# Linear-attention block with a gated MLP: keys of three chunks computed by features and transposed back by DMA

## The chip, the cores and the metric

The kernel runs on one core of a Trainium2 chip. The metric is the device time of one execution in microseconds (us). Engines: TensorE (PE) multiplies matrices into eight PSUM banks, VectorE (DVE), ScalarE (ACT) and GpSimd (POOL) do elementwise work, SyncE (SP) issues most DMAs. Each engine, and each DMA queue, takes its instructions in the order in which the program lists them; an instruction that waits holds up all behind it.

## The reference: what is computed

x has 2048 rows (tokens) of 640 features in bf16. The matmul operands are bf16 throughout.

```python
xn = layernorm(x)
# A: linear attention, 32 heads of 20 features
q, k, v = split(xn @ wqkv)
phi = lambda t: jnp.where(t > 0, t + 1, jnp.exp(t)) + 1e-6
pq, pk = phi(q), phi(k)
kv = einsum("bhsd,bhse->bhde", pk, v);   z = einsum("bhsd->bhd", pk)
num = einsum("bhqd,bhde->bhqe", pq, kv); den = einsum("bhqd,bhd->bhq", pq, z)[..., None] + 1e-6
s = (num / den) @ wo
# B: MLP, 640 -> 1728 -> 640
g = silu(relu(xn @ w1) @ w2)
out = x + s * g
```

## The kernel before

**Tiling.** Tokens stand in 16 tiles of 128 and in 4 chunks of 512 (J=4); features in 5 blocks of 128 (C=5); the MLP's 1728 hidden features in 13 blocks and one of 64. `xn` holds the normalised x by tokens, `xnT` its transpose by features, `pk` phi(k) by tokens, `pqT` phi(q) by features.

**Scheduling.** `Sched` keeps one list of operations per engine in program order and works out semaphore waits from the keys that each operation reads (R) and writes (W). A group of matmuls waits for all its inputs ahead of its first matmul. DMAs go to the queue named (nearly all to SP), also in program order. The order is written out by hand; there is no planner.

**Stage 0 (chunk 0).** x tiles are loaded and centred, transposed by PE into `xnT`, and the MLP's first hidden blocks are computed (`H_first`, `H_mm` L547, evicted by ACT in `H_ev` L554). The list `order` (L690) mixes key tiles ("K", 0..7), that is, chunks 0 and 1, with hidden blocks 5 to 12. Tiles from 4 on are normalised on DVE (`LN_stats`: statistics L397 and L399, inverse root on POOL L401 and L403; `LN_norm` L412) and transposed by an SP DMA (`xnT_dma` L455).

**A key tile** is `K_mm` (L464): ten matmuls, five blocks of features times two halves of 320 columns, into two banks. Then an exponential (L482, L485) and a relu (L491 to L499) of 640 columns, mostly on ACT, and two passes on DVE in `K_fin` (L505, L507), which write `pk[:, t, :]`. `z_add` (L473) adds each `pk` tile to `zacc` on POOL.

**The chunk loop j = 1, 2, 3 (L711).** For chunk j it computes five query blocks (`Q_block`: PE L532, ACT exponential L539, DVE pair L540 and L542) and 13 hidden blocks, in the order q h h q h h ... for j = 1 and 2: 18 blocks, n = 0 to 17. Both need `xnT` of chunk j. For chunk j+1 it does `LN_stats` after n = 0, 2, 4, 6, `LN_norm` and the transpose after n = 1, 3, 5, 7, and a key tile after n = 9, 12, 14, 17 into banks 0 and 1. Queries and hidden blocks take banks 2 to 7 in a ring (`nextb`). Loop j=3 also does chunk 0's queries from a second transpose of xn (`xq0`, L746, into the place of the key weights), sums z over tokens on PE (`z_split`, `z_col` L637), makes the block-diagonal `zmat` and the denominators (`den`, L650 to L658).

**After the loop.** SP issues, in this order: w2 (L766, L770), the reciprocals to DRAM (L773), their replicas back (L777, five loads of 512 KB). PE computes the key-feature product `G_block` (L792), GT = xn^T pk: five blocks of 32 matmuls of 320 columns, evicted by ACT (L797). `kv_block` (L803) multiplies the value weights by GT, after five matmuls of the MLP's second layer (`T_main`, L844); `W_block` (L814) folds in wo. `divide` (L783) divides `pqT` on DVE. The rest is the second MLP layer, the products with `wf` (L887, L922), silu and the output.

Of the kernel before, what the change touches and what calls it, by code (L numbers as in the profile page):

```python
# [211 lines left out]
def bass_recurrent_scan__linear_attn_block__dense_activation_relu__prompt_kernel(  # L212
# [87 lines left out]
    zmat = nc.alloc_sbuf_tensor("zmat", [P, C, H], bf)  # L300
    zacc = nc.alloc_sbuf_tensor("zacc", [P, D], f32)
    zhl = nc.alloc_sbuf_tensor("zhl", [P, 2, D], bf)
    mhalf = nc.alloc_sbuf_tensor("mhalf", [P, 1], f32)
# [12 lines left out]
    def ps2(b, n):  # L316
        return psT[:, 512 * b:512 * (b + 2)].rearrange("p (a n) -> p a n", a=2)[:, :, 0:n]

    done_sems = {E: nc.alloc_semaphore(f"done_{E}") for E in CENGS}
    NDS = 100  # L320
    dma_sems = [nc.alloc_semaphore(f"dsem{i}") for i in range(NDS)]
# [29 lines left out]
    sc.op("POOL", lambda eng: eng.memset(mhalf[:, :], -0.5), W=[("mhalf",)])  # L351
    sc.op("POOL", lambda eng: eng.memset(zacc[:, :], 0.0), W=[("zacc",)])

# [54 lines left out]
    def xnk(t, cs=range(C)):  # L408
        return [("xn", t, c) for c in cs]

    def LN_norm(t):
        last_norm[0] = sc.op("DVE", lambda eng: eng.tensor_scalar(  # L412
            out=xn[:, t, :], in0=xin[:, t % XR, :], scalar1=mv[:, t, 0:1], scalar2=rsy[:, t:t + 1],
            op0=ALU.subtract, op1=ALU.mult), R=[("xin", t % XR), ("mv", t), ("rsy", t)], W=xnk(t))
        if t + XR < T:
            x_load(t + XR)
# [51 lines left out]

    zpend = []

    def z_add():
        t = zpend.pop(0)
        sc.op("POOL", lambda eng: eng.tensor_tensor(out=zacc[:, :], in0=zacc[:, :], in1=pk[:, t, :], op=ALU.add),  # L473
              R=[("zacc",), ("pk", t)], W=[("zacc",)])

    def two(ap):
        return ap.rearrange("p (a n) -> p a n", a=2)

    def K_exp(t, b):
        e_ = two(ek[:, t % NEK, 0, :])  # L480
        if t < 4:
            sc.op("ACT", lambda eng: eng.activation(out=e_, in_=ps2(b, HN), func=ACTF.Exp, scale=rsy[:, t:t + 1]),  # L482
                  R=[("ps", b), ("ps", b + 1), ("rsy", t)], W=[("ek_e", t % NEK)])
        else:
            sc.op("ACT", lambda eng: eng.activation(out=e_, in_=ps2(b, HN), func=ACTF.Exp),  # L485
                  R=[("ps", b), ("ps", b + 1)], W=[("ek_e", t % NEK)])

    def K_relu(t, b):
        r_ = two(ek[:, t % NEK, 1, :])
        if t < 2:  # L490
            sc.op("DVE", lambda eng: eng.tensor_scalar(out=r_, in0=ps2(b, HN), scalar1=rsy[:, t:t + 1], scalar2=0.0,  # L491
                                                       op0=ALU.mult, op1=ALU.max),
                  R=[("ps", b), ("ps", b + 1), ("rsy", t), ("ek_e", t % NEK)], W=[("ek_r", t % NEK)])
        elif t < 4:
            sc.op("ACT", lambda eng: eng.activation(out=r_, in_=ps2(b, HN), func=ACTF.Relu, scale=rsy[:, t:t + 1]),
                  R=[("ps", b), ("ps", b + 1), ("rsy", t)], W=[("ek_r", t % NEK)])
        else:
            sc.op("ACT", lambda eng: eng.activation(out=r_, in_=ps2(b, HN), func=ACTF.Relu),  # L498
                  R=[("ps", b), ("ps", b + 1)], W=[("ek_r", t % NEK)])  # L499

    def K_fin(t):
        es = t % NEK
        e_ = ek[:, es, 0, :]
        r_ = ek[:, es, 1, :]
        sc.op("DVE", lambda eng: eng.tensor_scalar(out=e_, in0=e_, scalar1=1.0, scalar2=1e-6, op0=ALU.min, op1=ALU.add),  # L505
              R=[("ek_e", es)], W=[("ek_e", es)])
        sc.op("DVE", lambda eng: eng.tensor_tensor(out=pk[:, t, :], in0=e_, in1=r_, op=ALU.add),  # L507
              R=[("ek_e", es), ("ek_r", es)], W=[("pk", t)])
        zpend.append(t)

    def K_ev(t, b):
        K_exp(t, b)
        K_relu(t, b)
        K_fin(t)

# [3 lines left out]
    def nextb():  # L519
        b = RB[ring[0] % len(RB)]  # L520
        ring[0] += 1
        return b
# [106 lines left out]

    def z_split():  # L630
        sc.op("POOL", lambda eng: eng.tensor_copy(zhl[:, 0, :], zacc[:, :]), R=[("zacc",)], W=[("zhi",)])
        sc.op("POOL", lambda eng: eng.tensor_tensor(out=zhl[:, 1, :], in0=zacc[:, :], in1=zhl[:, 0, :], op=ALU.subtract),
              R=[("zacc",), ("zhi",)], W=[("zlo",)])

    def z_col():
        b = nextb()
        sc.group("PE", [(lambda eng, c=c, a=a: eng.matmul(ps[b][:, c:c + 1], lhsT=zhl[:, a, P * c:P * (c + 1)],  # L637
                                                          rhs=onesM[:, 0:1], start=(a == 0), stop=(a == 1)))
                        for c in range(C) for a in range(2)],
                 R=[("zhi",), ("zlo",), ("onesM",)], W=[("ps", b)])  # L640
        sc.op("DVE", lambda eng: eng.tensor_tensor(out=zmat[:, :, :], in0=mh[:, :, :],
                                                   in1=ps[b][:, 0:C].unsqueeze(2).to_broadcast([P, C, H]), op=ALU.mult),
              R=[("ps", b), ("mh",)], W=[("zmat",)])

# [18 lines left out]
    def K_step(t):  # L663
        b = (0, 6)[t % 2]
        K_mm(t, b)
        K_exp(t, b)
        if t == 0:
            LN_stats(4)
        K_relu(t, b)
        if t == 0:  # L670
            LN_norm(4)
            xnT_dma(4)
        if t == 1:
            LN_stats(5)
            K_fin(0)
            LN_norm(5)
            xnT_dma(5)
        if t >= 4:
            if t == 4:
                LN_norm(0)  # L680
                LN_norm(1)
            else:
                K_fin(t - 1)
            if t == 6:
                LN_norm(2)
                LN_norm(3)
            if t == 7:
                K_fin(t)

    order = [("K", 0), ("K", 1), 5, ("K", 2), 6, ("K", 3), 7, 8, ("K", 4), 9, ("K", 5), 10, ("K", 6), 11, ("K", 7), 12]  # L690
    for a in order:
        if isinstance(a, tuple):
            K_step(a[1])
        else:
            H_block(0, a, (2, 3, 4, 5)[(a - 5) % 4])
        if a == 6:
            LN_stats(6)
            K_fin(1)
            LN_norm(6)
            xnT_dma(6)  # L700
        if a == 8:
            LN_stats(7)
            K_fin(2)
            LN_norm(7)
            xnT_dma(7)
            K_fin(3)
    ring[0] = 0
    w_load(wv_sb[:, :, :], A_wqkv[:, 2 * D:3 * D], ("wv",))


    for j in range(1, J):  # L711
# [11 lines left out]
        for n, (kind, jj, f) in enumerate(blocks):  # L723
# [4 lines left out]
            if j + 1 < J:  # L728
# [3 lines left out]
                if n in (1, 3, 5, 7):  # L732
                    LN_norm(t0 + n // 2)
                    xnT_dma(t0 + n // 2)
                if n in (9, 12, 14, 17):
                    t = t0 + (9, 12, 14, 17).index(n)
                    K_mm(t, 0)
                    K_ev(t, 0)
                if n in (8, 10, 12, 14, 16):
                    z_add()  # L740
                if j == 1 and n == 16:
                    build_masks()
            else:
                if n == 0:
                    for t in range(4):
# [6 lines left out]
                        W=[("wo", 1)], extra=[last_norm[0]])  # L752
                if n % 2 == 0 and zpend:
                    z_add()
                    if not zpend:
                        z_split()
                if n == 18:
                    z_col()
                if n == 20:
                    den()  # L760
                    H_halves()
    assert not zpend

# [22 lines left out]


    def G_block(k, b):
        fns = []
        for t in range(T):  # L790
            for a in range(2):
                fns.append(lambda eng, t=t, a=a: eng.matmul(  # L792
                    ps[b + a][:, 0:HN], lhsT=xn[:, t, P * k:P * (k + 1)], rhs=pk[:, t, HN * a:HN * (a + 1)],
                    start=(t == 0), stop=(t == T - 1)))
        ag = sc.group("PE", fns, R=[kk for t in range(T) for kk in xnk(t)] + [("pk", t) for t in range(T)],
                      W=[("ps", b), ("ps", b + 1)])
        sc.op("ACT", lambda eng: eng.activation(out=two(GT[:, k, :]), in_=ps2(b, HN),  # L797
                                                func=ACTF.Copy), R=[("ps", b), ("ps", b + 1)], W=[("GT", k)])
        return ag

    def kv_block(c, b):
        n0 = V0[c]
        sc.group("PE", [(lambda eng, k=k: eng.matmul(ps[b][0:VR, 0:VR], lhsT=wv_sb[:, k, n0:n0 + VR],  # L803
                                                     rhs=GT[:, k, n0:n0 + VR], start=(k == 0), stop=(k == C - 1)))
                        for k in range(C)], R=[("wv",)] + [("GT", k) for k in range(C)], W=[("ps", b)])
        sc.op("DVE", lambda eng: eng.tensor_tensor(
# [142 lines left out]

    lastG = None  # L950
    for k in range(C):
# [117 lines left out]
```

## Time and profile before

| | |
|---|---|
| median of 3 runs | 221.4 us (220.67 to 221.53) |
| profiled execution, its own time | 220.62 us |
| its span | 218.9 us |
| PE clock granted | 1.00 |
| HBM read, written | 15.75 MB, 5.24 MB |

A row of a timeline is: start in us, length in us, engine, line of the code, operation, what it writes and reads, how many; in brackets how long the engine stood idle before and what released it. A row of the chain is start, length, engine and line. A group row is the line, engine and operation, the count, then busy time in us and mean ns of one. "DMA to landing" counts from the issue to the arrival of the last byte; x1, x2 or x5 is the number of issues. A matmul's own length is modelled and overlaps the next one's; the spacing in the chain is what it costs.

### The profile page before, as it was taken

Reading aid. Unit: us, or ns where it says so; the run is one execution under the profiler, and the core shown is the slowest. Engines: PE = TensorE matmul, PEld = TensorE weight load, DVE = VectorE, ACT = ScalarE, POOL = GpSimd, SP = SyncE. Lnnn points to the kernel's source line nnn. Section 1 sums busy time; section 2 is a strip of 40 time slices with the busy share of each in tenths; the row PEclk is TensorE's granted clock in tenths of the full one; section 3 lists DMA queues with packets and bytes.
Section 4 is the critical chain, followed back from the end, with each engine's and each line's share of the span. In section 5 each row is a group of like instructions: output and inputs, shape, how many; then the busy total and the mean of one; then the engine's idle time right before and its main releaser. Section 6 shows DMA issues by size and latency. Waiting matters only on the chain.

```text
span 218.9 us, 3262 instructions
## 1 busy us (share of the span) xinstructions
PE 214.4 (98%) x1318; PEld 118.3 (54%) x1318; DVE 113.9 (52%) x199; ACT 88.0 (40%) x147; POOL 43.5 (20%) x66
## 2 busy tenths in 40 slices
PE   7999999999999999999999999999999999999994
PEld 2975654555545554444467777534444446555573
DVE  2788846789676999987700006601121122460363
ACT  3587765567656666555321113614210311001120
POOL 2153101279023998700000000000000000000001
PEclk9999999999999999999999999999999999999999
DMA  6999581331013206800069959369212113342151
GB/s 205 294 377 189 121 240 36 61 54 8 0 30 60 33 1 120 168 3 0 0 194 364 275 172 371 90 206 316 48 24 48 24 27 73 76 157 89 38 180 63
DMA packets 36972, 26.46 MB, mean 121 GB/s; under 512 B 19973, under 2 KB 36317, under 8 KB 36957
## 3 DMA queue, kind: packets, MB, share of 16 engines
q1 hardware_dynamic: 36012, 25.50, 42.4%
q10 hardware_dynamic: 944, 0.75, 1.0%
q8 instruction: 10, 0.16, 0.3%
q14 instruction: 6, 0.04, 0.1%
HBM read 15.75 MB, written 5.24 MB: 96 GB/s over the span
## 4 chain that ended last, share of the span: by engine, by line
PE 96%; DMA 1%; DVE 1%; issue 0%
PE psT L547 26%; PE psT L844 19%; PE psT L464 10%; PE psT L792 10%; PE psT L532 10%; PE psT L887 7%; PE psT L851 7%; PE psT L922 2%; DMA reg<-in_A_x_dram 1%; PE psT L569 1%; PE psT L866 1%; PE psT L803 1%; PE psT L814 1%; PE psT L439 1%; PE psT L650 1%; DVE ek L426 0%
## 5 line engine op out<-in xcount | busy, mean ns | idle before, releaser
L547 PE MATMUL psT<-reg 128*128 128x512 bf16 (+1 forms) x335 | 61.7, 331 | 0.0
L844 PE MATMUL psT<-hT,reg 128*128 128x512 bf16 x195 | 44.6, 379 | 0.0
L547 PEld LDWEIGHTS psT<-reg 128*128 128x128 bf16 x335 | 28.5, 98 | 25.6 <-issue 0.4
L554 ACT ACTIVATE hT<-psT 128x512 bf16<-128x512 f32 x52 | 30.7, 600 | 15.8 <-PE psT L547 15.7
L894 DVE TENSOR_TENSOR er<-psT,ek 128x512 bf16<-128x512 f32 x15 | 10.4, 691 | 49.0 <-PE psT L887 49.0
L844 PEld LDWEIGHTS psT<-hT,reg 128*128 128x128 bf16 x195 | 18.9, 98 | 22.2 <-issue 0.7
L882 ACT ACTIVATE ek<-psT 128x512 bf16<-128x512 f32 x15 | 8.3, 599 | 42.3 <-PE psT L869 21.9
L929 POOL TENSOR_TENSOR reg<-reg 128x256 bf16<-128x256 bf16 x1 | 0.7, 666 | 123.8 <-DVE reg L937 123.8
L532 PE MATMUL psT<-reg 128*128 128x512 bf16 x100 | 24.9, 379 | 0.0
L464 PE MATMUL psT<-reg 128*128 128x320 bf16 x160 | 24.2, 299 | 0.0
L473 POOL TENSOR_TENSOR zacc<-zacc,reg 128x640 f32<-128x640 f32 x16 | 23.7, 1483 | 1.9 <-DVE reg L507 1.0
L792 PE MATMUL psT<-reg 128*128 128x320 bf16 x160 | 21.9, 299 | 0.0
L464 PEld LDWEIGHTS psT<-reg 128*128 128x128 bf16 x160 | 15.6, 98 | 8.2
L792 PEld LDWEIGHTS psT<-reg 128*128 128x128 bf16 x160 | 15.6, 98 | 6.2
L887 PE MATMUL psT<-pqT,reg 128*128 128x512 bf16 x75 | 18.1, 379 | 0.0
L542 DVE SCALAR_TENSOR_TENSOR pqT<-er 128x512 bf16<-128x512 bf16 x20 | 17.1, 854 | 0.7
L532 PEld LDWEIGHTS psT<-reg 128*128 128x128 bf16 x100 | 9.7, 98 | 11.6 <-DVE er L540 0.6
L539 ACT ACTIVATE er<-psT 128x512 bf16<-128x512 f32 x20 | 12.0, 598 | 8.9 <-PE psT L532 8.1
L851 PE MATMUL psT<-reg,hT 128*128 128x320 bf16 x104 | 15.3, 299 | 0.0
L540 DVE TENSOR_SCALAR er<-psT 128x512 bf16<-128x512 f32 x20 | 13.6, 678 | 3.1 <-ACT er L539 3.1
L507 DVE TENSOR_TENSOR reg<-ek 128x640 bf16<-128x640 bf16 x16 | 13.5, 843 | 1.5 <-ACT ek L498 1.0
L397 DVE BATCH_NORM_STATS2 stats<-reg 128x6 f32<-128x320 bf16 x32 | 13.9, 476 | 0.1
(71 smaller groups left out, 164.9 us busy)
## 6 DMA issues: line engine op xcount, KB each, us to landing
rscr<-rden SPq DMA_DIRECT2D x4, 640.0 KB, 10.5
reg<-rscr SPq DMA_DIRECT2D x5, 512.0 KB, 5.8
reg<-in_A_x_dram SPq DMA_DIRECT2D x4, 640.0 KB, 6.2
reg<-in_A_x_dram SPq DMA_DIRECT2D x15, 160.0 KB, 3.8
out_dram<-reg SPq DMA_DIRECT2D x15, 160.0 KB, 1.9
reg<-in_A_wqkv_dram SPq DMA_DIRECT2D x2, 800.0 KB, 6.6
reg<-in_B_w_dram SPq DMA_DIRECT2D x1, 1120.0 KB, 6.0
reg<-in_B_w_dram SPq DMA_DIRECT2D x1, 960.0 KB, 9.2
```

The source lines that it names most:

```text
L397: sc.op("DVE", lambda eng, a=a: eng.bn_stats(stats[:, t, a, :], xv[:, HN * a:HN * (a + 1)]), R=[("xin", t % XR)], W=[("stats", t, a)])
L464: fns.append(lambda eng, a=a, k=k: eng.matmul(ps[b + a][:, 0:HN], lhsT=xnT[:, k, tok(t)], rhs=wqk[:, k, D + HN * a:D + HN * (a + 1)], star ...
L473: sc.op("POOL", lambda eng: eng.tensor_tensor(out=zacc[:, :], in0=zacc[:, :], in1=pk[:, t, :], op=ALU.add), R=[("zacc",), ("pk", t)], W=[( ...
L532: sc.group("PE", [(lambda eng, k=k: eng.matmul(ps[b], lhsT=wqk[:, k, P * f:P * (f + 1)], rhs=rhs(k), start=(k == 0), stop=(k == C - 1))) f ...
L540: sc.op("DVE", lambda eng: eng.tensor_scalar(out=r_, in0=ps[b], scalar1=0.0, scalar2=1e-6, op0=ALU.max, op1=ALU.add), R=[("ps", b), ("er_e ...
L542: sc.op("DVE", lambda eng: eng.scalar_tensor_tensor(out=pqT[:, f, schunk(j)], in0=e_, scalar=1.0, in1=r_, op0=ALU.min, op1=ALU.add), R=[(" ...
L547: return sc.group("PE", [(lambda eng, k=k: eng.matmul(ps[b][:, lo:hi], lhsT=w1_sb[:, k, P * f:P * (f + 1)], rhs=xnT[:, k, 512 * j + lo:512 ...
L554: sc.op("ACT", lambda eng: eng.activation(out=hT[:, f, schunk(j)], in_=ps[b], func=ACTF.Relu), R=[("ps", b)], W=[("hT", j, f)])
L792: fns.append(lambda eng, t=t, a=a: eng.matmul(ps[b + a][:, 0:HN], lhsT=xn[:, t, P * k:P * (k + 1)], rhs=pk[:, t, HN * a:HN * (a + 1)], sta ...
L844: sc.group("PE", [(lambda eng, f=f: eng.matmul(ps[b], lhsT=w2_sb[:, f, P * m:P * (m + 1)], rhs=hT[:, f, schunk(j)], start=(f == 0 and not ...
L851: sc.group("PE", [(lambda eng, f=f: eng.matmul(ps[b][:, 0:HN], lhsT=hT[:, f, tok(t)], rhs=w2_sb[:, f, HN * n:HN * (n + 1)], start=(f == 0 ...
L887: sc.group("PE", [(lambda eng, c=c: eng.matmul(ps[b], lhsT=wf[:, c, P * m:P * (m + 1)], rhs=pqT[:, c, schunk(j)], start=(c == 0), stop=(c ...
```

## The change

Keys of chunk 0 stay as tiles by tokens. Keys of chunks 1 to 3 are computed by features: `KT_block(j, m)` multiplies the key weights of 128 features by 512 tokens of `xnT` (five matmuls of 512 columns, one bank of banks 0 and 1), takes phi there and sends the block back to token order in `pk` by a DMA transpose on SP. Since a feature's tokens now lie along a row, ACT sums them for z while copying (`K_sum`); chunk 0's keys are transposed by DMA into a part of `pqT` that is still free (`K0_turn`) and summed there (`K0_sum`). `z_all` adds the partial sums. POOL's additions, `z_split` and `z_col` go. In the product GT, key features 0 to 511 are done in one matmul of 512 columns per tile and block; the last 128 key features are done once with the roles of the operands exchanged (`G_rest`), evicted by ACT and transposed into GT by an SP DMA, for which `kv_block` now waits. Three of the fifteen blocks take their relu from ACT, the others from DVE. The transposes of xn are issued ahead of the load of the next x tile instead of behind it.

```diff
+    def KT_block(j, m, b, act=False):
+        lastK[0] = sc.group("PE", [(lambda eng, k=k: eng.matmul(
+            ps[b], lhsT=wqk[:, k, D + P * m:D + P * (m + 1)], rhs=xnT[:, k, schunk(j)],
+            start=(k == 0), stop=(k == C - 1))) for k in range(C)],
+            R=[("wk",)] + [kk for q in range(4) for kk in xtk(4 * j + q)], W=[("ps", b)])
+        es = kn[0] % NEK
+        kn[0] += 1
...
+        sc.op("ACT", lambda eng: eng.activation(out=e_, in_=ps[b], func=ACTF.Exp), R=[("ps", b)], W=[("ek_e", es)])
+        if act:
+            sc.op("ACT", lambda eng: eng.activation(out=r_, in_=ps[b], func=ACTF.Relu),
...
+        else:
+            sc.op("DVE", lambda eng: eng.tensor_scalar(out=r_, in0=ps[b], scalar1=0.0, scalar2=1e-6, op0=ALU.max,
+                                                       op1=ALU.add), R=[("ps", b), ("ek_e", es)], W=[("ek_r", es)])
+            sc.op("DVE", lambda eng: eng.scalar_tensor_tensor(out=e_, in0=e_, scalar=1.0, in1=r_, op0=ALU.min,
+                                                              op1=ALU.add),
+                  R=[("ek_e", es), ("ek_r", es)], W=[("ek_e", es)])
+        dma("SP", lambda eng: eng.dma_start_transpose(pk[:, 4 * j:4 * j + 4, P * m:P * (m + 1)], e_),
+            R=[("ek_e", es)], W=[("pkT", j, m)])
+        zs.append((j, m, e_, r_, es))
+    def K_sum():
+        j, m, e_, r_, es = zs.pop(0)
+        sc.op("ACT", lambda eng: eng.activation(out=r_, in_=e_, func=ACTF.Copy, accum_out=zk[:, j, m:m + 1]),
+              R=[("ek_e", es)], W=[("ek_r", es), ("zk", j, m)])
+    def K0_turn(t):
+        dma("SP", lambda eng: eng.dma_start_transpose(pqT[:, :, tok(t)], pk[:, t, :]), R=[("pk", t)],
+            W=[("pkf", t)])
...
         if t == 1:
             LN_stats(5)
+            LN_stats(6)
+            LN_norm(5, True)
+            LN_stats(7)
+            LN_norm(6, True)
             K_fin(0)
-            LN_norm(5)
-            xnT_dma(5)
...
+            LN_norm(7, True)
+            K_fin(1)
...
-    order = [("K", 0), ("K", 1), 5, ("K", 2), 6, ("K", 3), 7, 8, ("K", 4), 9, ("K", 5), 10, ("K", 6), 11, ("K", 7), 12]
+    order = [("K", 0), ("K", 1), 5, ("K", 2), 6, ("K", 3), 7, 8, 9, 10, 11, 12]
...
+    KT_block(1, 0, 0, True)
+    KT_block(1, 1, 1, True)
     ring[0] = 0
...
-                if n in (9, 12, 14, 17):
-                    t = t0 + (9, 12, 14, 17).index(n)
-                    K_mm(t, 0)
-                    K_ev(t, 0)
-                if n in (8, 10, 12, 14, 16):
-                    z_add()
+                if j == 1 and n in (1, 4, 7):
+                    KT_block(1, 2 + (1, 4, 7).index(n), kn[0] % 2, n == 1)
+                if n in (11, 13, 14, 16, 17):
+                    KT_block(j + 1, (11, 13, 14, 16, 17).index(n), kn[0] % 2)
+                if n in (0, 3, 6, 9, 10, 12, 13, 15, 16, 17) and zs and (n < 11 or len(zs) > 1):
+                    K_sum()
+                if j == 2 and n in (8, 10, 12, 14):
+                    K0_turn((8, 10, 12, 14).index(n))
...
+    def G_rest(b):
+        sc.group("PE", [(lambda eng, t=t, a=a: eng.matmul(
+            ps[b + a][:, 0:HN], lhsT=pk[:, t, KW:D], rhs=xn[:, t, HN * a:HN * (a + 1)],
+            start=(t == 0), stop=(t == T - 1))) for t in range(T) for a in range(2)],
+            R=xnall + pkk, W=[("ps", b), ("ps", b + 1)])
+        grk = [("er_e", 0), ("er_r", 0)]
+        sc.op("ACT", lambda eng: eng.activation(out=two(gr), in_=ps2(b, HN), func=ACTF.Copy),
+              R=[("ps", b), ("ps", b + 1)], W=grk)
+        dma("SP", lambda eng: eng.dma_start_transpose(GT[:, :, KW:D], gr), R=grk, W=[("GTr",)])
     def G_block(k, b):
...
+        ag = sc.group("PE", [(lambda eng, t=t: eng.matmul(
+            ps[b][:, 0:KW], lhsT=xn[:, t, P * k:P * (k + 1)], rhs=pk[:, t, 0:KW],
+            start=(t == 0), stop=(t == T - 1))) for t in range(T)], R=xnall + pkk, W=[("ps", b)])
...
-                        for k in range(C)], R=[("wv",)] + [("GT", k) for k in range(C)], W=[("ps", b)])
+                        for k in range(C)], R=[("wv",), ("GTr",)] + [("GT", k) for k in range(C)], W=[("ps", b)])
...
-    lastG = None
+    G_rest(6)
     for k in range(C):
         lastG = G_block(k, (0, 2)[k % 2])
```

More of the change, by code (lines that the diff above doesn't have):

```diff
@@ L300, in bass_recurrent_scan__linear_attn_block__dense_activation_relu__prompt_kernel @@
     zmat = nc.alloc_sbuf_tensor("zmat", [P, C, H], bf)
-    zacc = nc.alloc_sbuf_tensor("zacc", [P, D], f32)
-    zhl = nc.alloc_sbuf_tensor("zhl", [P, 2, D], bf)
+    zk = nc.alloc_sbuf_tensor("zk", [P, 7, C], f32)
     mhalf = nc.alloc_sbuf_tensor("mhalf", [P, 1], f32)
@@ L414, in LN_norm @@
             op0=ALU.subtract, op1=ALU.mult), R=[("xin", t % XR), ("mv", t), ("rsy", t)], W=xnk(t))
+        if turn:
+            xnT_dma(t)
         if t + XR < T:
@@ L467, in K_mm @@
         lastK[0] = sc.group("PE", fns, R=xtk(t, ks) + [("wk",)], W=[("ps", b + a) for a in halves])
[L469 to L474, printed above, removed]
     def two(ap):
@@ L480, in K_exp @@
         e_ = two(ek[:, t % NEK, 0, :])
[L481 to L486, printed above, removed]
+        sc.op("ACT", lambda eng: eng.activation(out=e_, in_=ps2(b, HN), func=ACTF.Exp, scale=rsy[:, t:t + 1]),
+              R=[("ps", b), ("ps", b + 1), ("rsy", t)], W=[("ek_e", t % NEK)])
     def K_relu(t, b):
@@ new lines, in bass_recurrent_scan__linear_attn_block__dense_activation_relu__prompt_kernel, with K0_sum @@
+    zs = []
+    def K_sum():
[5 more added lines that the diff above has]
+            W=[("pkf", t)])
+    def K0_sum(m):
+        sc.op("ACT", lambda eng: eng.activation(out=pqT[:, m, schunk(0)], in_=pqT[:, m, schunk(0)], func=ACTF.Copy,
+                                                accum_out=zk[:, 0, m:m + 1]),
+              R=[("pkf", t) for t in range(4)], W=[("pqT", 0, m), ("zk", 0, m)])
@@ L516, in bass_recurrent_scan__linear_attn_block__dense_activation_relu__prompt_kernel @@
+    sc.allow_unread.update([("ek_r", i) for i in range(NEK)] + [("pqT", 0, m) for m in range(C)])
     RB = [2, 3, 4, 5, 6, 7]
@@ L628, in bass_recurrent_scan__linear_attn_block__dense_activation_relu__prompt_kernel, with z_all @@
     H_first(3, (4, 0, 1, 2, 3))
[L630 to L640, printed above, removed]
+    def z_all():
+        for o, a, b in ((4, 0, 1), (5, 2, 3), (6, 4, 5)):
+            sc.op("DVE", lambda eng, o=o, a=a, b=b: eng.tensor_tensor(out=zk[:, o, :], in0=zk[:, a, :], in1=zk[:, b, :],
+                                                                      op=ALU.add),
+                  R=[("zk", q, m) for q in (a, b) for m in range(C)], W=[("zk", o, m) for m in range(C)])
         sc.op("DVE", lambda eng: eng.tensor_tensor(out=zmat[:, :, :], in0=mh[:, :, :],
-                                                   in1=ps[b][:, 0:C].unsqueeze(2).to_broadcast([P, C, H]), op=ALU.mult),
-              R=[("ps", b), ("mh",)], W=[("zmat",)])
+                                                   in1=zk[:, 6, :].unsqueeze(2).to_broadcast([P, C, H]), op=ALU.mult),
+              R=[("zk", 6, m) for m in range(C)] + [("mh",)], W=[("zmat",)])
     def den():
@@ L670, in K_step @@
         if t == 0:
[L671 to L672 removed]
+            LN_norm(4, True)
         if t == 1:
             LN_stats(5)
+            LN_stats(6)
+            LN_norm(5, True)
+            LN_stats(7)
+            LN_norm(6, True)
             K_fin(0)
[L676 to L690 removed]
+            LN_norm(7, True)
+            K_fin(1)
+    order = [("K", 0), ("K", 1), 5, ("K", 2), 6, ("K", 3), 7, 8, 9, 10, 11, 12]
     for a in order:
@@ L695, in bass_recurrent_scan__linear_attn_block__dense_activation_relu__prompt_kernel @@
             H_block(0, a, (2, 3, 4, 5)[(a - 5) % 4])
[L696 to L700, printed above, removed]
+        if a == 7:
+            K_fin(2)
         if a == 8:
[L702 to L705, printed above, removed]
+            LN_norm(0)
+            LN_norm(1)
             K_fin(3)
+        if a == 9:
+            LN_norm(2)
+            LN_norm(3)
+    KT_block(1, 0, 0, True)
+    KT_block(1, 1, 1, True)
     ring[0] = 0
@@ L752, in bass_recurrent_scan__linear_attn_block__dense_activation_relu__prompt_kernel @@
                         W=[("wo", 1)], extra=[last_norm[0]])
[L753 to L758, printed above, removed]
+                if zs:
+                    K_sum()
+                elif n in (3, 4, 5, 6, 7):
+                    K0_sum(n - 3)
+                if n == 12:
+                    z_all()
                 if n == 20:
@@ L761, in bass_recurrent_scan__linear_attn_block__dense_activation_relu__prompt_kernel @@
                     H_halves()
-    assert not zpend
+    assert not zs
     for a in range(2):
@@ L785, in divide @@
                           R=[("rep", m)] + [("pqT", i, m) for i in range(J)], W=[("pqT", i, m) for i in range(J)]))
-    def G_block(k, b):
[L789 to L798, printed above, removed]
+    KW = D - P
+    pkk = [("pk", t) for t in range(4)] + [("pkT", j, m) for j in range(1, J) for m in range(C)]
+    xnall = [kk for t in range(T) for kk in xnk(t)]
+    gr = er[:, :, :, :].rearrange("p a b n -> p (a b n)")[:, 0:D]
+    def G_rest(b):
[7 more added lines that the diff above has]
+        dma("SP", lambda eng: eng.dma_start_transpose(GT[:, :, KW:D], gr), R=grk, W=[("GTr",)])
+    def G_block(k, b):
+        ag = sc.group("PE", [(lambda eng, t=t: eng.matmul(
+            ps[b][:, 0:KW], lhsT=xn[:, t, P * k:P * (k + 1)], rhs=pk[:, t, 0:KW],
+            start=(t == 0), stop=(t == T - 1))) for t in range(T)], R=xnall + pkk, W=[("ps", b)])
+        sc.op("ACT", lambda eng: eng.activation(out=GT[:, k, 0:KW], in_=ps[b][:, 0:KW], func=ACTF.Copy),
+              R=[("ps", b)], W=[("GT", k)])
         return ag
```

26 lines of the change are left out of this document (12 added, 14 removed).

## The prediction

> **What bounds the kernel now.** I read the shares of busy time first, then the chain of waits in order of time, then the timelines of VectorE (DVE) and of SyncE's DMA queue (SP) in the stretches that the change rewrites.
>
> ```profile
> PE 214.4 (98%) x1318; PEld 118.3 (54%) x1318; DVE 113.9 (52%) x199; ACT 88.0 (40%) x147; POOL 43.5 (20%) x66
> PE 96%; DMA 1%; DVE 1%; issue 0%
> ```
>
> TensorE (PE) is busy for 98% of the span, and 96% of the chain that ends last is PE. So only two things can move the time: PE work that disappears, and new times in which PE waits. Relief on another engine is worth nothing by itself.
>
> ```profile
> 12.22 2.72 PE psT L464 x20
> ...
> 31.72 1.08 PE psT L532 x5
> ...
> 56.58 1.08 PE psT L532 x5
> ...
> 102.00 0.23 PE psT L637 x10
> ...
> 110.17 21.73 PE psT L792 x160
> ...
> 132.99 1.65 PE psT L803 x30
> ```
>
> Columns are start, length, line. A block of five matmuls of 512 columns (L532) takes 1.08 us, ten of 320 columns (L464) 1.36. Chunk loop j=1 begins at 31.72, j=2 at 56.58. The key-feature product (L792) runs from 110.17, and L803 at 132.99 is its first reader.
>
> **PE work removed.** Keys of chunks 1 to 3: before 12 tiles x 1.36 = 16.32 us, after 15 blocks x 1.08 = 16.20; both are 38,400 columns. The product: 160 matmuls at 21.73/160 = 0.136 become 80 at 0.216 (1.08/5) and 32 at 0.136, 17.28 + 4.35 = 21.63. The column sum of z, L637, goes: 0.23. Together 0.12 + 0.10 + 0.23 = 0.45 us less, 0.2% of the time. Everything else of the change is off PE, so the rest is a search for new PE waits.
>
> **Engines that get lighter or heavier.** POOL loses the 16 additions of z.
>
> ```profile
> 70.78 14.12 POOL L473 TENSOR_TENSOR zacc<-zacc,reg 128x640 f32<-128x640 f32 x9
> L507 DVE TENSOR_TENSOR reg<-ek x16: 491/493/1617, 18.0 to 85.5; 128x640 bf16<-128x640 bf16 x16
> 32.00:57.00 25.00, 25.00 (x132) 12.81 (x131) 19.47 (x33) 15.17 (x26) 12.11 (x19) 1.00 0.23 46
> 57.00:81.00 24.00, 24.00 (x127) 12.22 (x125) 19.94 (x32) 15.13 (x26) 12.87 (x15) 1.00 0.17 28
> 81.00:110.00 29.00, 29.00 (x169) 13.00 (x167) 24.78 (x28) 15.41 (x26) 9.53 (x7) 1.00 0.28 55
> ```
>
> The key sum (L507; minimum, median, maximum in ns) takes 0.49 us mostly and up to 1.6; I put the difference down to the additions. But the three window rows (length, then busy time of PE, PEld, DVE, ACT, POOL, then clock, DMA share, GB/s) show PE busy for all of each stretch, so a lighter DVE frees nothing on the path. ScalarE (ACT) loses 24 exponentials and relus of 640 columns and gains 15 exponentials and 3 relus of 512 columns at 0.60 (L554) and 20 sums, which I price at the same 0.60 plus 0.19 to read the accumulator: 10.8 + 15.8 = 26.6.
>
> ```profile
> L554 ACT ACTIVATE hT<-psT 128x512 bf16<-128x512 f32 x52 | 30.7, 600 | 15.8 <-PE psT L547 15.7
> L422 ACT ACTIVATION_READ_ACCUMULATOR ek<-reg 128x1 f32 x3 | 0.6, 188 | 0.0
> ```
>
> Even without counting what it loses, this fits into the (25 - 15.2) + (24 - 15.1) + (29 - 15.4) = 32 us that ACT has free there, so I take zero. A sum that waits for DVE holds up the evictions behind it, but the ring of six banks covers some 5 us of that; without the cover PE would wait as long as the sum does.
>
> **First new wait: keys of chunk 3 in loop j=2.** A key tile needed one transposed tile of xn; a key block of 512 columns needs all four of its chunk. Before, the tiles came after n=9, 12, 14 and 17 of the loop. Now the first block comes after n=11 and needs tile 15.
>
> ```profile
> 58.44 0.69 DVE L540 TENSOR_SCALAR er<-psT 128x512 bf16<-128x512 f32 x1
> ...
> 61.89 0.45 DVE L412 TENSOR_SCALAR reg<-reg,mv,rsy 128x640 bf16<-128x640 bf16 x1 [1.00 <-POOL rsy L403]
> ...
> 70.85 1.51 DVE L412 TENSOR_SCALAR reg<-reg,mv,rsy 128x640 bf16<-128x640 bf16 x1 [0.99 <-POOL rsy L403]
> ```
> ```profile
> L455 SPq DMA_TRANSPOSE reg<-reg x12: 1199/1200/2108, 16.1 to 72.4; - x12
> DMA to landing us min/median/max: 2.6/2.7/4.0
> ```
> ```profile
> 20.31 0.27 DVE L505 TENSOR_SCALAR ek<-ek 128x640 bf16<-128x640 bf16 x1
> ```
> ```profile
> 33.47 0.69 DVE L540 TENSOR_SCALAR er<-psT 128x512 bf16<-128x512 f32 x1 [0.90 <-ACT er L539]
> ...
> 42.44 0.68 DVE L540 TENSOR_SCALAR er<-psT 128x512 bf16<-128x512 f32 x1
> 43.15 0.69 DVE L542 SCALAR_TENSOR_TENSOR pqT<-er 128x512 bf16<-128x512 bf16 x1
> 43.77 0.88 DVE L397 BATCH_NORM_STATS2 stats<-reg 128x6 f32<-128x320 bf16 x2
> ...
> 45.88 1.51 DVE L412 TENSOR_SCALAR reg<-reg,mv,rsy 128x640 bf16<-128x640 bf16 x1 [1.00 <-POOL rsy L403]
> ```
>
> DVE does query pairs, statistics and norms in program order and waits about 1 us for POOL's inverse root ahead of a norm (the bracket at L412). Tile 15's norm starts at 70.85, 14.27 us after the loop's start. The order of these operations stays, and POOL's additions begin only at 70.78, so nothing ahead of that gets faster. The last key block ahead of the loop delays DVE a little: its pair costs what a query pair does, 43.77 - 42.44 = 1.33, and ends about 0.7 + 1.33 = 2.0 us after PE, where the loop's first query operation began 58.44 - 56.58 = 1.86 after: +0.17. The norm then takes 0.45, as tile 12's does at 61.89 without the additions, and the transpose 2.6 to land: 14.27 + 0.17 + 0.45 + 0.05 + 2.6 = 17.5 us. PE arrives after 12 blocks, 12.95. **Wait: 4.6 us.** Bounds: 4.0, if DVE starts half a microsecond sooner, and 6.0, if the transpose takes the 4.0 of the slowest.
>
> **Second: keys of chunk 2 in loop j=1.** The same, with three blocks of chunk 1 ahead. From the first query operation to tile 11's norm it is 45.88 - 33.47 = 12.41 us. Between them now stand the pair of the block after n=1, 0.27 + 0.49 at 640 columns, so about 0.6 at 512, and that of the block after n=4, 1.33, of which 1.0 fills a wait for POOL: +0.95. The loop starts four tiles and ten blocks after 12.22, at 28.46, and its first query operation comes 33.47 - 31.72 = 1.75 later, at 30.2. So the norm is at 43.55, the landing at 46.65, and PE is there after 15 blocks, at 44.66. **Wait: 2.0 us**, bounds 1.0 and 3.4. SP gets 20 more transposes, of 1.2 us each to issue, but they are spread over 80 us, and none stands late ahead of tile 11 or 15.
>
> ```profile
> 16.61 0.88 DVE L397 BATCH_NORM_STATS2 stats<-reg 128x6 f32<-128x320 bf16 x2
> ```
>
> Tile 7, for the first key block of all at 26.30, starts from the statistics of tile 5 at 16.61: three sets of 1.1, norms and one key sum ahead of the last norm, end near 22, landing near 25: no wait. The loads of wv and x, pushed behind transposes on SP, are needed later than they land by several microseconds. In j=3 the four query transposes (L746) queue behind the last key transpose, 1.2 us each: 2.0 + 5 x 1.2 + 1.4 to land = 9.4 us after the loop's start against ten blocks, 10.8; without that cover it costs a microsecond at most.
>
> **Third: the exchanged product.** Its 128 columns are evicted some 5 us into the product, but their transpose stands on SP behind everything issued since the loop, and the first kv block (L803) now waits for it.
>
> ```profile
> 128.59 2.28 SPq L777 DMA_DIRECT2D reg<-rscr  x5
> L777 SPq DMA_DIRECT2D reg<-rscr x5: 355/432/453, 128.6 to 130.4; - x5
> DMA to landing us min/median/max: 3.3/5.8/8.3
> ```
>
> SP stands at L777 until the reciprocals are in DRAM, so it issues the transpose at 130.87 at the earliest; PE wants it at 132.99 - 0.10 = 132.89. Alone it would land at 130.87 + 2.6 = 133.5, 0.6 us late. But five loads of 512 KB lie ahead, whose landings spread from 128.6 + 3.3 = 131.9 to 130.4 + 8.3 = 138.7, 1.7 us apart. The transpose moves 160 KB; behind them at the same rate it lands near 138.7 + 0.5 = 139.2. **Wait: 6.3 us**, bounds 0.6 and 138.7 + 2.6 - 132.9 = 8.4. I take the queued value, since those loads, issued 0.45 us apart, land one behind another. On PE the W blocks and the rest wait behind kv, on DVE the five divisions; all move with it. [...]
>
> **The sum.** -0.45 + 2.0 + 4.6 + 6.3 = +12.45 us. The profiled execution took 220.62 us (span 218.9), 0.8 under the median of 221.4; it becomes 233.1. From the median it would be 233.9. I say 233.3.
>
> **Rivals.** (1) PE's clock falls in the long gaps, 0.27.
>
> ```profile
> 0.83 3.65 PE L357 MATMUL psT<-const-bfloat16-1.0 128*128 128x512 bf16 x9 [0.83 <-PEq L1054]
> ```
>
> At the start, after idling, nine matmuls of 512 columns took 3.65 us, 0.41 each against 0.216: 3.65 - 9 x 0.216 = 1.7 us lost. If a gap of 4.6 or 6.3 us brings that back, each adds 1.7: 234.8 for one, 236.5 for both. Against it, no later gap of this trace is long enough to show it. [...]
>
> (2) The transpose overtakes the loads, and kv waits 0.6 to 2 us: 220.62 - 0.45 + 2.0 + 4.6 + 0.6 = 227.4, up to 229. For it speaks only that it is small. 0.12.
>
> (3) DVE, freed of POOL's additions, keeps ahead of PE, and only the third wait stays: 226.5. Against it, the additions do not touch the stretch that matters. 0.06.
>
> (4) Not slower: all three transposes land before their readers. It decides at tile 15: its norm would have to end 10.3 us after the loop's start instead of 14.9, and the exchanged columns would have to pass SP's blocked issue. Then only the 0.45 us remain: 220.2, which a measurement cannot tell from no change. 0.05, of which 0.02 for a gain over 0.5%, if ends of other gaps close too.
>
> The forecast itself has 0.50, 231.0 to 235 by the bounds of the first two waits and most of the third's. The range reaches into the second rival and over both cases of the first: 228.0 to 236.8. A measurement of this kernel can tell about 0.5%, 1.1 us. Faster 0.02, same 0.03, slower 0.95.
>
> **What would show it.** In the profile after, PE's matmul time should hardly move while its gaps grow by about 13 us at three places: ahead of the first key block after n=11 of loops 1 and 2, with the transpose of xn as releaser, and at the first kv matmul, with that of the exchanged columns. DVE's query operations should lose their values above 1 us. If matmuls after a gap take 0.41 us, the first rival holds; if kv starts within 2 us of the matmuls ahead of it, the second. If loops 1 and 2 show no gap, my reading of DVE's order is wrong.

## The result, and the profile after

The change is slower: 239.1 us median of 6 runs (238.1 to 241.7) against 220.9, a ratio of 1.082 (95% interval 1.077 to 1.086). The forecast was 233.3 in a range of 228.0 to 236.8; the sign and the three waits came as forecast, the time lies above the range. In the change, in three experiments and in the kernel before, single executions took more than 1.5% longer than the fastest of the same kernel (at the most 830.6 us, in e5, and 381.6, in e10), and the ratios leave these out.

From the page of the profiled execution (238.09 us, span 236.0):

```profile
PE 218.6 (93%) x1215; PEld 110.8 (47%) x1215; DVE 108.1 (46%) x208; ACT 94.6 (40%) x182; POOL 16.8 (7%) x47
PEclk9999999999999799999999998699999999999999
PE 75%; DVE 12%; issue 4%; DMA 4%; POOL 2%; ACT 1%
```

PE's share fell from 98% to 93%. The clock row, all nines before, has two dents, in slices 14 and 25 to 26 of 40. The chain now leaves PE for DVE, DMA and "issue". Who PE waited for (total, times, longest):

```profile
PE psT L502 <- DMA reg<-reg: 7.2, 3, 4.5
PE psT L833 <- issue: 6.3, 1, 6.3
```

L502 is the key block, L833 the first kv matmul. The releaser "issue" in the second row means that the profile found none; that it is the transpose follows below from its landing. Now the chain in order of time around the waits:

```profile
44.25 0.45 DVE reg L411
44.72 2.58 DMA reg<-reg
47.35 1.25 PE psT L502 x5
...
58.31 1.09 PE psT L502 x5
...
73.81 0.45 DVE reg L411
74.28 2.56 DMA reg<-reg
76.89 2.17 PE psT L502 x5
79.07 1.85 PE psT L564 x5
80.91 1.08 PE psT L579 x5
...
119.08 4.35 PE psT L814 x32
123.42 17.27 PE psT L824 x80
140.69 1.08 PE psT L874 x5
141.77 6.28 issue
148.04 3.22 PE psT L833 x30
```

In loop j=2, which starts at 58.31 + 1.09 = 59.40, tile 15's norm (L411) starts 14.4 us later and its transpose lands at 76.84, and only then the key block runs. It takes 2.17 us where the same block takes 1.08 or 1.09 elsewhere and 1.25 behind the gap of loop j=1, the query block behind it takes 1.85, and the next is back at 1.08. The kv matmuls take 3.22 us, against 1.65 before. Here is the clock around the gap of loop j=2, and last around that at kv (stretch, its length, busy time of PE, PEld, DVE, ACT, POOL, then granted clock, DMA share, GB/s):

```profile
74.00:76.00 2.00, 0.00 (x0) 0.00 (x0) 1.55 (x3) 0.00 (x0) 0.00 (x0) 1.00 0.27 55
76.00:77.00 1.00, 0.11 (x1) 0.11 (x2) 0.00 (x0) 0.00 (x0) 0.00 (x0) 1.00 0.46 93
77.00:78.00 1.00, 1.00 (x3) 0.31 (x3) 0.00 (x0) 0.00 (x0) 0.00 (x0) 0.54 0.64 126
78.00:79.00 1.00, 1.00 (x4) 0.44 (x3) 0.00 (x0) 0.00 (x0) 0.00 (x0) 0.50 0.82 164
79.00:80.00 1.00, 1.00 (x4) 0.32 (x3) 0.27 (x1) 0.60 (x1) 0.00 (x0) 0.50 0.00 0
80.00:81.00 1.00, 1.00 (x5) 0.38 (x4) 0.97 (x2) 0.05 (x1) 0.00 (x0) 0.76 0.00 0
81.00:82.00 1.00, 1.00 (x6) 0.46 (x5) 0.57 (x2) 0.55 (x1) 0.00 (x0) 1.00 0.00 0
...
145.00:147.00 2.00, 0.00 (x0) 0.00 (x0) 0.00 (x0) 0.00 (x0) 0.00 (x0) 0.59 1.04 371
...
152.00:153.00 1.00, 1.00 (x6) 0.63 (x5) 1.00 (x2) 0.54 (x1) 0.00 (x0) 0.92 0.00 0
```

A stretch of 1 us at 0.54 is half clock for 0.92 of it, so the clock is half from about 77.1 to 80.5, 3.4 us. At kv it is half from about 145.4, still inside the gap, to 152.2, of which 4.1 us are work. It costs (2.17 - 1.08) + (1.85 - 1.08) = 1.9 us in loop j=2, of which 0.17 is what the block behind the gap of loop j=1 also took longer, at full clock. At kv it costs 2.1: from kv's start to L874's long run it is 157.94 - 148.04 = 9.90 us, before 140.81 - 132.99 = 7.82. The transpose of the exchanged columns (L821), and the five loads ahead of it (L796):

```profile
L821 SPq DMA_TRANSPOSE reg<-er x1: 1321/1321/1321, 140.8 to 140.8; - x1
DMA to landing us min/median/max: 7.1/7.1/7.1
L796 SPq DMA_DIRECT2D reg<-rscr x5: 356/432/466, 138.5 to 140.3; - x5
DMA to landing us min/median/max: 3.4/5.2/6.9
```

It lands at 140.85 + 7.1 = 147.95, 0.1 us ahead of kv; the last load lands near 140.3 + 6.9 = 147.2.

### The profile page after: what moved, and what is told of

Same layout as the page of the kernel before. It is cut to its first block, busy times and chain, and to the rows that moved or that the text cites. A ratio compares the mean times of both kernels' runs of the same rounds, so it can differ in the third digit from the quotient of the medians.

```text
span 236.0 us, 3093 instructions
## 1 busy us (share of the span) xinstructions
PE 218.6 (93%) x1215; PEld 110.8 (47%) x1215; DVE 108.1 (46%) x208; ACT 94.6 (40%) x182; POOL 16.8 (7%) x47
## 4 chain that ended last, share of the span: by engine, by line
PE 75%; DVE 12%; issue 4%; DMA 4%; POOL 2%; ACT 1%
PE psT L874 18%; PE psT L579 13%; PE psT L824 7%; PE psT L917 7%; PE psT L881 6%; PE psT L564 6%; PE psT L502 6%; DMA reg<-reg 4%; DVE stats L396 4%; PE psT L952 2%; PE psT L814 2%; DVE reg L411 2%; DVE pqT L574 2%; PE psT L356 2%; POOL rsy L402 2%
## 5 line engine op out<-in xcount | busy, mean ns | idle before, releaser
L874 PE MATMUL psT<-hT,reg 128*128 128x512 bf16 x195 | 44.8, 381 | 0.0
L579 PEld LDWEIGHTS psT<-reg 128*128 128x128 bf16 x335 | 28.6, 98 | 27.6 <-issue 0.7
L924 DVE TENSOR_TENSOR er<-psT,ek 128x512 bf16<-128x512 f32 x15 | 10.4, 692 | 49.5 <-PE psT L917 49.5
L874 PEld LDWEIGHTS psT<-hT,reg 128*128 128x128 bf16 x195 | 19.0, 98 | 22.7 <-issue 1.0
L502 PE MATMUL psT<-reg 128*128 128x512 bf16 x75 | 19.4, 394 | 7.2 <-DMA reg<-reg 7.2
L564 PE MATMUL psT<-reg 128*128 128x512 bf16 x100 | 25.7, 388 | 0.0
L912 ACT ACTIVATE ek<-psT 128x512 bf16<-128x512 f32 x15 | 8.3, 598 | 42.3 <-PE psT L899 21.9
L824 PE MATMUL psT<-reg 128*128 128x512 bf16 x80 | 17.4, 379 | 0.0
L836 DVE TENSOR_TENSOR reg<-psT,m 120x120 bf16<-120x120 f32 x6 | 1.7, 283 | 31.2 <-PE psT L833 31.2
L564 PEld LDWEIGHTS psT<-reg 128*128 128x128 bf16 x100 | 10.1, 100 | 12.6 <-issue 1.4
L502 PEld LDWEIGHTS psT<-reg 128*128 128x128 bf16 x75 | 7.2, 100 | 17.2 <-DMA reg<-reg 8.7
L519 DVE TENSOR_SCALAR ek<-psT 128x512 bf16<-128x512 f32 x12 | 8.2, 687 | 13.9 <-ACT ek L510 13.9
L510 ACT ACTIVATE ek<-psT 128x512 bf16<-128x512 f32 x15 | 9.0, 597 | 13.7 <-PE psT L502 13.7
L574 DVE SCALAR_TENSOR_TENSOR pqT<-er 128x512 bf16<-128x512 bf16 x20 | 13.8, 692 | 0.7
L881 PEld LDWEIGHTS psT<-reg,hT 128*128 128x128 bf16 x104 | 10.1, 98 | 4.8 <-issue 0.3
```

Of the source, the lines that this page charges most:

```text
L502: lastK[0] = sc.group("PE", [(lambda eng, k=k: eng.matmul(ps[b], lhsT=wqk[:, k, D + P * m:D + P * (m + 1)], rhs=xnT[:, k, schunk(j)], star ...
L564: sc.group("PE", [(lambda eng, k=k: eng.matmul(ps[b], lhsT=wqk[:, k, P * f:P * (f + 1)], rhs=rhs(k), start=(k == 0), stop=(k == C - 1))) f ...
L574: sc.op("DVE", lambda eng: eng.scalar_tensor_tensor(out=pqT[:, f, schunk(j)], in0=e_, scalar=1.0, in1=r_, op0=ALU.min, op1=ALU.add), R=[(" ...
L579: return sc.group("PE", [(lambda eng, k=k: eng.matmul(ps[b][:, lo:hi], lhsT=w1_sb[:, k, P * f:P * (f + 1)], rhs=xnT[:, k, 512 * j + lo:512 ...
L824: ag = sc.group("PE", [(lambda eng, t=t: eng.matmul(ps[b][:, 0:KW], lhsT=xn[:, t, P * k:P * (k + 1)], rhs=pk[:, t, 0:KW], start=(t == 0), ...
L874: sc.group("PE", [(lambda eng, f=f: eng.matmul(ps[b], lhsT=w2_sb[:, f, P * m:P * (m + 1)], rhs=hT[:, f, schunk(j)], start=(f == 0 and not ...
```

## The experiments

The theory after the result (A): each long gap of PE costs its own length and then about 2 us of matmuls at half clock. Its rivals: (B) the gaps cost only their length, and the rest comes from heavier DMA or ACT work; at kv (C) PE waits for something else than the transpose.

**Transpose of the exchanged columns early (e1).** The exchanged product and its transpose are written ahead of the reciprocals' write:

```diff
+    G_rest(6)
     for i in range(J):
         dma("SP", lambda eng, i=i: eng.dma_start(
             rscr[:, schunk(i)]...
-    G_rest(6)
     for k in range(C):
         lastG = G_block(k, (0, 2)[k % 2])
```

> The transpose of the exchanged columns is issued on SP ahead of the reciprocals' write and the five loads, so it lands early in the product. Theory A (each long gap costs its length and then about 2 us of matmuls at half clock): the 6.3 us gap at kv and its 2 us go, 239.1 - 8.3 = about 231. Theory B (only the gap's length counts, the rest of the loss is heavier DMA or ACT work): 239.1 - 6.3 = about 233. Rival C (kv waits for something else, the transpose is only the last to arrive): no less than 237.

Measured: 231.5 us, ratio 1.048 (1.044 to 1.053). The chain at kv (L835 here):

```profile
142.01 1.08 PE psT L876 x5
143.09 1.65 PE psT L835 x30
```

No gap, and kv at 1.65 us again. That is 7.6 us less than the change, nearer to A's 8.3 than to B's 6.3; the interval, about 230.8 to 232.8 us, reaches to both, so here it is the profile, and not the time, that speaks for A. C is out.

**Norms early (e2).** Statistics and norms of the next chunk move ahead, the last norm from n=7 to n=3:

```diff
-                if n in (0, 2, 4, 6):
-                    LN_stats(t0 + n // 2)
-                if n in (1, 3, 5, 7):
-                    LN_norm(t0 + n // 2, True)
+                if n < 2:
+                    LN_stats(t0 + 2 + n)
+                if n < 4:
+                    LN_norm(t0 + n, True)
+                if j == 1 and n in (15, 17):
+                    LN_stats(12 + (n - 15) // 2)
...
+    LN_stats(8)
+    LN_stats(9)
     ring[0] = 0
```

> The kv wait stays; the statistics and norms of the next chunk are pulled ahead, so that its last transpose lands before the first key block (my count: DVE reaches norm 11 about 4 us and norm 15 about 6 us sooner). Theory A: gaps of 2.2 and 4.5 us and 1.9 us at half clock go, 239.1 - 8.6 = about 230.5. Theory B: 239.1 - 6.7 = about 232.4. If DVE's order is not the cause: still over 237.

Measured: 231.0 us, ratio 1.044 (1.040 to 1.048): 8.1 us less, by A's 8.6 and above B's 6.7. Both gaps of the loops are gone; what is left is kv's:

```profile
133.47 7.16 issue
140.63 3.23 PE psT L837 x30
```

This gap is 0.9 us longer than the change's, so by estimate the transpose took 7.1 + 0.9 = 8.0 us to land, and the half clock behind it lasts to 146.3, for 5.7 us of work.

**Both (e3).** The two edits together, with what is left of the change.

> Both edits. Theory A: everything but tile 7's 0.5 us gap goes and the 0.45 us of PE work stays saved: 220.9 - 0.45 + 0.5 = about 221, the same as the kernel before, clock 1.00 throughout. Theory B: about 225, a rest of some 4 us that no gap explains.

Measured: 221.3 us, ratio 1.003 (1.000 to 1.006), as A said. The key blocks wait 0.3 us in all, for tile 7:

```profile
PE psT L502 <- DMA reg<-reg: 0.3, 1, 0.3
```

So nothing but the gaps and what follows them made the change slow, and with them gone it is not faster either. B's rest of 4 us is not there. A clock of 1.00 throughout, as A said, came in ten of the twelve executions only. The profiled one, 223.4 us, is not among them: near its start PE stood idle for 0.4 and then for 1.10 us, and the clock is 0.50 from 6.96 to 10.4 us.

```profile
6.77 3.21 PE L579 MATMUL psT<-reg 128*128 128x128 bf16 x30 [1.10 <-ACT ek L423]
```

Its mean clock is 0.992. The kernel before, run beside it, has an execution of 223.4 us with the same mean clock, so this is not the change's doing.

**Idle matmuls in two gaps (e4).** The waits stay; PE multiplies ones meanwhile, into a free bank:

```diff
+                if j == 2 and n == 11:
+                    fill(20, b=kn[0] % 2)
                 if n in (11, 13, 14, 16, 17):
...
+    fill(28, b=3)
     for c in range(VC):
         kv_block(c, c % 4)
```

> No wait is removed. 20 idle matmuls of ones stand ahead of the first key block of chunk 3 and 28 ahead of kv, about 4.3 and 6.0 us, just inside the gaps of 4.5 and 6.3 us; they compute nothing that is used. Theory A: the clock stays at 1.00 and about 4 us come back, 235, though PE does more. Theory B: 239, no change or a little slower.

Measured: 237.5 us, ratio 1.077 (1.073 to 1.081), between the two. Its profile says why. After both filled gaps the blocks keep their speed, but now the unfilled gap of 2.2 us in loop j=1 is followed by slow blocks (PE's timeline, in brackets the idle time ahead):

```profile
48.32 1.25 PE L502 MATMUL psT<-reg 128*128 128x512 bf16 x5 [2.20 <-DMA reg<-reg]
49.41 2.15 PE L564 MATMUL psT<-reg 128*128 128x512 bf16 x5
51.35 2.07 PE L579 MATMUL psT<-reg 128*128 128x512 bf16 x5
```

In the profile of the change the same gap had no such tail. The next run fills all three.

**Idle matmuls in three gaps (e8).** As e4, with nine more ahead of chunk 2's first key block:

```diff
+                if n == 11:
+                    fill((9, 20)[j - 1], b=kn[0] % 2)
```

> The change with idle matmuls of ones in all three gaps (9 ahead of chunk 2's first key block, 20 ahead of chunk 3's, 28 ahead of kv); the waits stay, what the idle matmuls compute is not used. Theory A (clock): the clock holds 1.00 after the gaps, 221 - 0.45 + 0.5 + 2.2 + 4.5 + 6.3 = about 234, and the runs spread less than the 3.6 us of the change. Theory B: 239 and the same spread.

Measured: 235.5 us, ratio 1.068 (1.064 to 1.071), five runs from 235.4 to 236.7, all at a mean clock of 1.00. PE does 57 matmuls more, waits as late as before for its data, and the kernel is 3.6 us faster than the change and spreads over 1.3 us in place of 2.2 (the change's five that the ratio counts, 238.1 to 240.3). That is the clock's part, shown by itself. The level is 1.5 us above my 234. Of that 0.35 is time outside the span, which the sum left out, and 0.7 is at kv, where PE still stood idle when the fill was done: by estimate the transpose took 7.8 us to land in place of 7.1. The rest is open. What the fills left idle:

```profile
PE psT L835 <- issue: 0.8, 1, 0.8
PE psT L502 <- DMA reg<-reg: 0.7, 3, 0.2
```

**Which gaps halve the clock (e5, e9).** 16 and 15 idle matmuls at the head of the gaps leave idle stretches of three lengths.

```diff
+                if j == 2 and n == 11:
+                    fill(16, b=kn[0] % 2)
...
+    fill(15, b=3)
```

> 16 idle matmuls at the head of the gap ahead of chunk 3's first key block and 15 at the head of that at kv, which leaves idle about 1.1 us there and 3.1 us at kv, beside the 2.2 us of loop j=1. [...] If a gap of 2 to 3 us can do it, depending on where it falls, the half clock shows after some: 234 to 238, with the gap of 1.1 us never followed by it.

Measured: ratio 1.086 (1.081 to 1.092), from 239.1 to 242.0 us, above what I expected. The profile, of the execution of 830.6 us, shows none of the three gaps, so the same kernel was run once more.

> The same kernel again, since the first one's profile shows a PE at a quarter of its speed throughout and says nothing of the gaps. Idle stretches of about 2.2 us (loop j=1), 1.1 us (loop j=2) and 3.1 us (kv). [...] If gaps of 2 to 3 us are enough, one or two of them are followed by some 4 us at half clock, each 2 us of loss: 237.5 to 239.5.

Measured: 239.9 us, ratio 1.086 (1.080 to 1.092), a little above the 237.5 to 239.5 expected with one or two tails. PE's timeline:

```profile
47.33 1.25 PE L502 MATMUL psT<-reg 128*128 128x512 bf16 x5 [2.20 <-DMA reg<-reg]
48.42 2.24 PE L564 MATMUL psT<-reg 128*128 128x512 bf16 x5
50.46 1.97 PE L579 MATMUL psT<-reg 128*128 128x512 bf16 x5
...
78.57 1.25 PE L502 MATMUL psT<-reg 128*128 128x512 bf16 x5 [1.06 <-DMA reg<-reg]
79.66 1.24 PE L564 MATMUL psT<-reg 128*128 128x512 bf16 x5
...
149.15 3.23 PE L835 MATMUL psT<-reg,wv_sb 128*120 128x120 bf16 x30 [4.11 <-issue]
```

The gap of 1.06 us has no tail, that of 4.11 has one, and that of 2.20 has one too, which begins only with the second block, when PE had been at work again for over a microsecond:

```profile
46.00:48.00 2.00, 0.67 (x4) 0.32 (x5) 1.30 (x3) 1.21 (x3) 0.25 (x2) 1.00 0.69 139
48.00:50.00 2.00, 2.00 (x7) 0.74 (x6) 0.71 (x2) 0.60 (x1) 0.00 (x0) 0.63 0.00 0
50.00:52.00 2.00, 2.00 (x6) 0.76 (x5) 1.34 (x2) 0.60 (x1) 0.00 (x0) 0.52 0.04 9
```

At kv PE stood idle for 4.1 us and not 3.1: kv came 8.63 us after the start of L876's five matmuls, in the change 7.51 us after that of L874's, so by estimate the transpose took 7.1 + 1.1 = 8.2 us to land. Cutting the idle time to about half without filling the gaps gained nothing over the change.

The clock rows show one regularity more, for which no run was made. In the change's profile, read in steps of 0.1 us, the clock is at half from 77.07 to 80.49 and from 145.34 to 152.17 us, that is, for 3.41 and for 6.83 us, twice as long. The rows of the others give 3.4 us in e1, e3, e4 and e9 (the two rows above: 1.48 + 1.92), 6.8 at e9's kv and 10.3 in e2. What sets these lengths is not shown, and neither is what sets the two gaps of 2.2 us that have a tail, in e4 and e9, apart from the two without one, in the change and e1; no run moved a gap.

**What the transpose waits for (e6).** It still waits for the reciprocals in DRAM, but is issued ahead of the five loads:

```diff
-        dma("SP", lambda eng: eng.dma_start_transpose(GT[:, :, KW:D], gr), R=grk, W=[("GTr",)])
+        dma("SP", lambda eng: eng.dma_start_transpose(GT[:, :, KW:D], gr),
+            R=grk + [("rscr", i) for i in range(J)], W=[("GTr",)])
+    G_rest(6)
     for c in range(C):
         dma("SP", lambda eng, c=c: eng.dma_start(rep[:, c, :], rscr[P * c:P * (c + 1), :]),
...
-    G_rest(6)
     for k in range(C):
```

> The transpose still waits until the reciprocals have landed in DRAM, as SP's queue made it wait, but it is issued ahead of the five loads instead of behind them. Theory Q (the wait at kv is the queue of five loads): the transpose lands 2.6 us after its issue, about when PE arrives, so the 6.3 us gap shrinks to under 1 us and the half clock behind it goes: about 231.5, like the kernel with the early transpose. Theory I (the late issue costs most of it, or a transpose beside the loads is slow): the gap stays at 3 us or more, 235 or over.

Measured: 230.6 us, ratio 1.043 (1.040 to 1.046). SP's timeline, the transpose's landing, and PE's chain:

```profile
139.71 1.22 SPq L808 DMA_TRANSPOSE reg<-er  x1
```
```profile
DMA to landing us min/median/max: 2.6/2.6/2.6
```
```profile
141.60 1.08 PE psT L876 x5
142.68 1.65 PE psT L835 x30
```

Issued at 139.71, it lands at 142.3, and kv starts at 142.68 without a gap, although the loads run beside it. So SP's blocked issue alone would have cost nothing; the whole wait comes from the five loads ahead in the queue. Counted from the product's start, they put the transpose's issue off by 2 us (140.85 - 119.08 = 21.8 us in the change, 139.71 - 119.98 = 19.7 here), and then it takes 7.1 us to land in place of 2.6.

**The exchanged product alone (e7).** The kernel before with `G_rest`, the 512-column `G_block` and the late transpose only.

> The kernel before with the exchanged product alone, its transpose behind the loads as in the change; keys and z as before. If the third wait is independent of the rest: 221.1 - 0.1 + 6.3 + 2.0 = about 229.3, with one gap, at kv. If the transposes of the keys or the sums on ACT had a part in that wait: less than 227.

Measured: 228.2 us, ratio 1.034 (1.030 to 1.039). The chain:

```profile
132.98 5.29 issue
138.27 3.23 PE psT L813 x30
```

7.2 us more than before, where I expected 8.2: the gap is 5.3 us this time, with the same tail; the transpose again took 7.1 us to land. The third wait needs nothing of the key change.

**Semaphores (e10).** All executions of the kernels that contain the key change take 2.0 to 2.2 us more than their spans, those of before 1.7.

```diff
-    NDS = 100
+    NDS = 124
```

> The kernel before with 124 DMA semaphores allocated in place of 100, the added 24 never used. The change's executions last 2.07 us longer than their spans, those of before 1.72. If the number of allocated semaphores sets that, it is 2.07 here too and the time 0.35 us longer; if it is the change's instructions, waits or DMAs, it stays at 1.72 and the time is the same.

Measured: ratio 0.9995 (0.997 to 1.002), and 1.7 us outside the span. e7 has 1.7 as well. So the 0.35 us come with the key part, and not from allocated semaphores; which of its DMAs or waits makes them stays open.

## Why the prediction was wrong

**The step that failed** is the treatment of the first rival, "PE's clock falls in the long gaps, 0.27": I kept it out of the sum because no later gap of the trace before was long enough to show it (PE's longest wait there is 0.6 us). That was no evidence against it, and my own sum made the very gaps that were missing. The same trace had one row that bore on it, nine matmuls at 0.41 us at the start; the granted clock reads 1.00 over them, so what slows them there is not shown. With the rival's 1.7 us for each of two gaps the sum was 236.5; the tails measured 1.9 and 2.1. Of the 5.0 us from the sum, 233.1, to the profiled 238.09, these tails are 4.0, tile 7's wait 0.5, the time outside the span 0.35 and the first wait 0.2. The top of the range, 236.8, had room for both tails only with every wait at its middle value. The clock rows of the runs show the drop to 0.50 behind the gaps of 4.55 and 6.28 us; 2.2 us idle was enough in two profiles, e4 and e9, and there the tail began after PE had restarted, at 49.6 against 48.32 and at 48.52 against 47.33.

**The three waits held.** Loop j=2: 4.6 forecast, 4.55 measured, from a norm 14.4 us after the loop's start (14.44 forecast). Loop j=1: 2.0 and 2.2. At kv: 6.3 and 6.28; the landing was put at 29.0 us after the product's start and came at 147.95 - 119.08 = 28.9. e6 shows the mechanism as argued, queued behind the loads, and against the second rival. e2 shows that it was DVE's order that made the first two, against the third rival.

**PE's work**: the product took 4.35 + 17.27 = 21.62 us, as worked out; the block of 512 columns 1.08. e3, without the waits, is at best equal to the kernel before: 0.45 us less on PE, against 0.35 more outside the span and tile 7's wait.

**Tile 7** was taken as no wait; it is 0.47 us in the change. The transpose was issued at 22.82, 0.8 us later than I put it, and took 3.8 us to land, where I took about 3. The row gave 4.0 as the slowest, but that one was issued at 16.1; those of the kernel before at 22.4 and 25.1 landed in 2.8. What slowed this one is open.

**DVE and ACT**: the query operations lost their slow values as forecast (L574 now 691 to 693 ns in all 20, before up to 1457), and this brought no time; ACT's added work cost none that e3 could show.

**The rest.** 13.5 us of gaps, 4.0 of half clock, 0.35 outside the span, less 0.45, make 17.4; the profiled executions differ by 238.09 - 220.62 = 17.5. The medians differ by 18.3, since the profiled execution is the change's fastest. A third drop of the clock, after the gap of loop j=1 as in e4 and e9, could lengthen others: an execution of 240.3 us has a mean clock of 0.971 against 0.978, and 0.007 of 236 us is 1.7 us, as much as 3.4 us at half clock take away. Where that drop lay is not shown. Two executions of 239.0 and 239.3 us have the same mean clock as the profiled one, and what makes them longer is open.

## What to carry to other kernels

Where PE is busy for nearly all of the span, a gap that a change opens can cost more than its length: here gaps of 4.55 and 6.28 us cost 1.9 and 2.1 us more, and one of 2.2 us had such a tail in e4 and e9 and none in the change and e1. So hold a tail of some 2 us possible behind such gaps, by estimate from these numbers, and give the rival its place in the sum when your own working creates the condition for it. A block that takes four tiles at once needs the last of them, so its place in the order has to be checked against the last producer's queue, not the first's. A transpose that was issued behind five loads of 512 KB on the same queue landed behind them, after 7.1 us in place of 2.6; where it stood in the queue was worth more here than the work that the change saved.

## What the runs showed of the hardware

**Where the granted clock fell.** It fell from 1.00 to 0.50 at 77.07 and 145.34 us in the change's profile, 4.7 and 3.6 us after PE went idle. By the rows of 2 us of the others it was 3.5 us after in e4, and 3.4 and 2.5 in e9. In e4 and in the first of e9's PE had been at work again for 1.3 and 1.2 us.

**How long it stayed there.** 3.41 and 6.83 us in the change; by the rows 3.4 in e1, e3 and e4, 3.4 and 6.8 in e9, 10.3 in e2. Of that 3.4 to 5.7 us (the change, e2, e9) were work behind the gap, and half of this, 1.7 to 2.8 us, is by estimate what each such gap lost beside its length.

**Behind which gaps.** Of those of 1.0 to 1.2 us the one in e3 (1.10, close behind one of 0.4) had such a tail, those in e1 (1.2), e4 (1.0) and e9 (1.06) had none. Of those of 2.2 us the ones in e4 and e9 had it, those in the change and e1 not. Of the longer ones it came behind both in the change (4.55 and 6.28), and in e1 (4.5), e2 (7.16), e7 (5.29, where kv took 3.23 us against 1.65 before) and e9 (4.11).

**The transpose and the loads.** A DMA transpose with 2.6 MB of loads issued behind it landed in 2.6 us (e6), the median of xn's transposes in the change. Issued behind those loads it took 7.1 us in the change and in e7, and by estimate from the longer waits at kv 7.8 in e8, 8.0 in e2 and 8.2 in e9.
